# Two decoder layers over a cached attention: one ring of four equal places for the weights, the first MLP in two column halves, and values that are given up by quarters

## The chip, the core and the metric

The kernel runs on one core of a Trainium2 chip. The core has five engines, each with its own queue of instructions: PE (TensorE, matrix products into PSUM), DVE (VectorE), ACT (ScalarE), POOL (GpSimd) and SP (SyncE), which here only issues transfers. Sixteen DMA engines move data between the chip's memory (HBM) and the on-chip memory (SBUF, 128 partitions). Engines wait for each other, and for transfers, on semaphores.

The metric is the device time of one execution in microseconds. Before the change the median of three runs is 2713.64 us (2713.55 to 2716.07).

## The reference

Two sublayers, an attention over a key and value cache and a gated MLP, are run twice with the same weights and caches:

```python
def _A_ref(x, k_cache, v_cache, wq, wo):          # x: (2, 1, 576); caches: (2, 32, 8192, 128)
    q = (x @ wq).reshape(B, Sq, H, Dh).transpose(0, 2, 1, 3)
    scores = jnp.einsum("bhqd,bhkd->bhqk", q, k_cache) * (Dh ** -0.5)
    p = _softmax(scores, axis=-1)
    o = jnp.einsum("bhqk,bhkd->bhqd", p, v_cache)
    return o.transpose(0, 2, 1, 3).reshape(B, Sq, H * Dh) @ wo

def _B_ref(x, w_gate, w_up, w_down):               # 576 -> 4608 -> 576
    return _gelu(x @ w_gate) * (x @ w_up) @ w_down

x = x + _A_ref(_layernorm(x), ...)
x = x + _B_ref(_layernorm(x), ...)
x = x + _A_ref(_layernorm(x), ...)
x = x + _B_ref(_layernorm(x), ...)
```

Everything is 32-bit float. The caches are 2 x 268 MB and are read in both layers; the weights are about 51 MB a layer.

## The kernel before

**Items.** The 2 x 32 pairs of batch and head are 64 items. An item's keys are 8192 x 128, laid out as 128 partitions of 64 rows each, 32 KB a partition, 4 MB in all; its values the same. The first layer takes the items forward, the second backward. The last two items' keys and the last three items' values stay in SBUF between the layers (`keys_held`, `values_held`, five slots) and are not read again.

**Space.** One tile, `space`, holds all that is loaded: six slots of 8192 columns (32 KB a partition each) and 1024 columns more. `Arena` hands it out while the program is written: `slot` for a whole item, `quarter` for a quarter of one, `ring` for pieces of weights, first fit from the end of the last piece. `cache`, `eighths`, `down`, `out_rows` and `products` put loads into one list, `queue`, in the order of use; `pump` issues the head of the list on SP as soon as the planner finds room for it, and stops where it does not. `done` frees a piece and pumps. SP then waits at run time until the old contents have been used, and everything behind it in the list waits too.

**Between the layers.** With five slots held, the first layer's output projection and MLP and the second layer's W_q have only the last slot and the 1024 columns, 9216 columns in all, from `RING` on. Pieces there are 2304 columns (W_o; gate and up, 9216 bytes a partition), 1728 (W_down in thirds, three rows of 576) and 2048 (W_q). So four to five pieces are loaded ahead.

**Attention** (`attention`, line 370). For item n, DVE multiplies a quarter of the keys by the query in place (line 413), POOL folds it in half (417), DVE adds it up (422) and the quarter is given up (`done`, 430). `peak` (436, a transpose on PE), `highest` (442) and `softmax` (448, 451) belong to item n - 1 and are written between the quarters of item n; then `total` (457) and `values` (472, 32 matmul instructions in the profile), after which the four quarters of the value slot are given up together. In the second layer the third item's keys go by quarters into the ring's slot as the W_q pieces there are used up, and the fourth's and fifth's by quarters into the two held key slots; all others are loaded whole.

**MLP** (`mlp`, line 575). All gate pieces, then all up pieces, each of four and a half rows a partition in nine pieces, accumulate into two banks of PSUM (line 584), columns being spread over four groups of partitions and two banks. Then the results are scaled by the norm's factor (591, 592), spread by 18 small matmuls with a selecting matrix so that hidden units lie on partitions (598), activated (605 to 610) and written to `hT` (612). Then W_down goes piece by piece (620) into `xps`, and x is updated (367). `norm` (341 to 364) stands ahead of each sublayer.

In the second layer the weights may use all of `space` (`weights_at[1]` is 0), so they are loaded far ahead.

Of the kernel before, what the change touches and what calls it, by code (L numbers as in the profile page):

```python
# [15 lines left out]
P = 128  # L16
# [15 lines left out]
EG = DF // 8  # L32
HG = EG // 2
# [7 lines left out]
END = NSLOT * SLOT + 1024  # L41
RING = 5 * SLOT
HELD = 5


class Arena:


    def __init__(self):
        self.live = {}  # L50
        self.freed = [0] * (NSLOT + 1)
        self.clock = 0
        self.at = RING

    def clear(self, lo, n):
        return all(hi <= lo or l >= lo + n for l, hi in self.live.values())

    def slot(self, key, allowed):

        for s in sorted(allowed, key=lambda s: self.freed[s]):  # L60
            if self.clear(s * SLOT, SLOT):
                for k in range(4):
                    self.quarter(key, s * SLOT, k)
                return s * SLOT
        return None

    def quarter(self, key, at, k):
        lo = at + k * PART
        if not self.clear(lo, PART):
            return False  # L70
        self.live[key, k] = (lo, lo + PART)
        return True

    def ring(self, key, n, lo, hi=None):

        for at in [self.at, lo] + sorted(end for _, end in self.live.values()):
            if lo <= at and at + n <= (hi or END) and self.clear(at, n):
                self.live[key] = (at, at + n)
# [12 lines left out]
def decode_layers(ctx, tc, x_in, kc, vc, wq, wo, wg, wu, wd, out):  # L91
# [23 lines left out]
    queue, ready, slots = [], {}, {}  # L115

    def pump():
        while queue:
            t = queue[0][1]()
            if t is None:  # L120
                return
            ready[queue.pop(0)[0]] = t
# [5 lines left out]
    def cache(key, src, hb, allowed, pieces=1, where=None):  # L128

        rows = src[hb % B, hb // B].rearrange("(p j) d -> p j d", p=P)  # L130

        def load(at, lo, hi):
            t = space[:, at:at + SLOT].rearrange("p (j d) -> p j d", d=DH)
            nc.sync.dma_start(t[:, lo:hi, :], rows[:, lo:hi, :])
            return t

        def make():
            at = arena.slot(key, allowed)
            if at is None:
                return None  # L140
            slots[key] = at
            for lo in range(0, J, J // pieces):
                t = load(at, lo, lo + J // pieces)
            return t

        def make_quarter(k):
            at = slots[key] = RING if where == "ring" else slots[where]
            return load(at, k * JC, (k + 1) * JC) if arena.quarter(key, at, k) else None

        if where is None:  # L150
            queue.append((key, make))
        else:

            for k in ((NU + i) % 4 if where == "ring" else i for i in range(4)):
                queue.append((key, lambda k=k: make_quarter(k)))

    def eighths(key, w, us, width, lo, hi=None):

        n = 4 * len(us)

        def make():
            at = arena.ring(key, n * width, lo, hi)
            if at is None:
                return None
            t = space[:, at:at + n * width].rearrange("p (c w) -> p c w", c=n)
            src = w.rearrange("r (e w) -> (r e) w", w=width).rearrange("(p j) w -> p j w", p=P)
            nc.sync.dma_start(t, src[:, 4 * us[0]:4 * us[0] + n, :])
            return t

        queue.append((key, make))  # L170


    ONE = [range(u, u + 1) for u in range(NU)]
    THREE = [range(u, u + 3) for u in range(0, NU, 3)]
    PIECES = {
        ("wq", 0): THREE, ("wq", 1): ONE, ("g", 0): ONE, ("u", 0): ONE, ("g", 1): THREE, ("u", 1): THREE[:-1] + ONE[-3:],
    }

    def down(key, t0, lo, hi, first):

        def make():
            at = arena.ring(key, (hi - lo) * D, first)
            if at is None:
                return None
# [478 lines left out]
```

## Time and profile before

| | |
|---|---|
| median of the runs | 2713.64 us |
| the profiled execution, its own time | 2714.15 us |
| its span, first to last instruction | 2712.4 us |
| mean granted TensorE clock | 0.651 |
| busy: PE, DVE, POOL, ACT | 1144.8, 1887.3, 1209.4, 82.6 us |
| read from HBM | 1154.23 MB |

The profile comes from one execution. An engine is busy while it runs an instruction that computes; waiting and issuing are not counted. The page cuts the span into forty slices of 67.8 us and gives for each the busy tenths and the data rate. A table of stretches gives the same for any part of the span. In a timeline, each row has its start and length in us, the engine, the line of the kernel, what was done and how often, and in brackets the idle time of the engine before it and what ended it. "space<-in_B_w_up_dram" reads: into `space`, from the tensor of the up weights.

### The profile page before, as it was taken

The page shows a single profiled execution, that of the slowest core. Times are in us where ns is not written, and L with a number is a line of the kernel's source. Part 1 is how long each engine was busy: PE and PEld are TensorE (multiplying, and loading weights), DVE is VectorE, ACT ScalarE, POOL GpSimd, SP SyncE. Part 2 cuts the span into 40 slices and gives each one's busy share as a digit, 9 for nine tenths or more (in the row PEclk, how much of TensorE's full clock was granted, in tenths as well). Part 3 has the DMA queues.
Part 4 walks back from the last instruction along what each step waited for, and adds up shares of the span by engine and source line. Part 5 has one row for each costly group of instructions (what it writes and reads, how often), then busy time and mean ns, then how long its engine had stood idle before and what let it go on. Part 6 is the DMA issues. An engine that isn't in the chain of part 4 may idle for free.

```text
span 2712.4 us, 19378 instructions
## 1 busy us (share of the span) xinstructions
PE 1144.8 (42%) x7392; PEld 406.0 (15%) x7392; DVE 1887.3 (70%) x1809; ACT 82.6 (3%) x391; POOL 1209.4 (45%) x522
## 2 busy tenths in 40 slices
PE   2344434343434343444555434343434343434356
PEld 0111111111111111111211111111111111111122
DVE  5777777777777777776039877777777777777740
ACT  0000000000000000000000000000000000000000
POOL 3545454444445454443016554444444454445420
PEclk7666666666666666666757766666666666566667
DMA  9999999999999999999999999999999999999998
GB/s 418 432 433 431 431 430 431 432 432 431 430 432 432 431 431 431 431 432 414 404 358 409 430 431 432 432 431 430 431 431 432 431 430 431 432 431 431 432 426 378
DMA packets 49099, 1155.48 MB, mean 426 GB/s; under 512 B 5464, under 2 KB 5488, under 8 KB 7664
## 3 DMA queue, kind: packets, MB, share of 16 engines
q1 hardware_dynamic: 48968, 1154.24, 99.4%
q8 instruction: 58, 0.95, 0.1%
q14 instruction: 33, 0.27, 0.0%
q10 hardware_dynamic: 40, 0.01, 0.0%
HBM read 1154.23 MB, written 0.00 MB: 426 GB/s over the span
## 4 chain that ended last, share of the span: by engine, by line
DMA 80%; DVE 10%; PE 8%; issue 2%; POOL 0%; ACT 0%; DVEq 0%; POOLq 0%; SPq 0%; ACTq 0%
DMA space<-in_A_k_cache_dram 45%; DMA space<-in_A_v_cache_dram 28%; PE acc L472 7%; DVE space L413 5%; DVE S L422 3%; DMA space<-in_B_w_down_dram 2%; DMA space<-in_B_w_gate_dram 2%; DMA space<-in_A_wo_dram 1%; DMA space<-in_B_w_up_dram 1%; DMA space<-in_A_wq_dram 1%; DVE osb L489 1%; PE xps L620 0%; PE acc L584 0%; PE acc L377 0%; POOL space L417 0%
## 5 line engine op out<-in xcount | busy, mean ns | idle before, releaser
L417 POOL TENSOR_TENSOR space<-space 128x1024 f32<-128x1024 f32 x512 | 1206.4, 2356 | 1257.1 <-DVE space L413 1221.7
L413 DVE TENSOR_TENSOR space<-space,qp 128x2048 f32<-128x2048 f32 x512 | 1164.7, 2275 | 483.8 <-DMA space<-in_A_k_cache_dram 460.9
L472 PE MATMUL acc<-space,prz 128*8 128x512 f32 x4096 | 727.4, 874 | 290.1 <-DVE osb L489 170.6
L422 DVE TENSOR_REDUCE S<-space 128x16 f32<-128x1024 f32 x512 | 615.9, 1203 | 3.3 <-POOL space L417 3.3
L438 PE MATMUL mT<-ident,m 128*1 128x128 f32 x128 | 46.7, 365 | 794.2 <-DVE m L436 794.2
L472 PEld LDWEIGHTS acc<-space,prz 128*8 128x8 f32 x4096 | 133.7, 115 | 771.4 <-issue 723.5
L444 PE MATMUL nb<-m,ones 1*128 1x1 f32 x256 | 74.1, 356 | 254.8 <-DVE m L442 254.8
L438 PEld LDWEIGHTS mT<-ident,m 128*1 128x1 f32 x128 | 10.1, 79 | 820.0 <-DVE m L436 814.0
L457 PE MATMUL tot<-rs,ones 128*128 128x1 f32 x256 | 74.7, 361 | 92.7 <-ACT prz L451 92.7
L444 PEld LDWEIGHTS nb<-m,ones 1*128 1x128 f32 x256 | 63.1, 305 | 291.4 <-DVE m L442 291.4
L448 ACT ACTIVATE nbs<-nb 128x1 f32<-128x1 f32 x128 | 21.9, 171 | 2359.9 <-PE nb L444 2359.9
L503 DVE TENSOR_TENSOR oT<-po,rinv 32x16 f32<-32x16 f32 x64 | 10.9, 170 | 110.7 <-PE po L498 110.7
L363 POOL TENSOR_TENSOR rstd<-ve,mhalf 128x1 f32<-128x1 f32 x4 | 2.2, 552 | 174.0 <-DVE ve L361 174.0
L457 PEld LDWEIGHTS tot<-rs,ones 128*128 128x128 f32 x256 | 63.7, 309 | 104.0 <-ACT prz L451 103.5
L396 PE MATMUL qp<-qsb,pick 4*128 4x128 f32 x256 | 62.3, 325 | 27.9 <-DVE space L413 24.8
L584 PE MATMUL acc<-space,xt 128*8 128x288 f32 x576 | 56.3, 545 | 39.9 <-DMA space<-in_B_w_up_dram 19.9
L489 DVE SCALAR_TENSOR_TENSOR osb<-acc,diag,osb 128x128 f32<-128x128 f32 x192 | 67.3, 351 | 6.8
L592 DVE TENSOR_SCALAR o<-acc,rstd 128x288 f32<-128x288 f32 x2 | 1.0, 516 | 94.1 <-ACT o L591 94.1
L396 PEld LDWEIGHTS qp<-qsb,pick 4*128 4x128 f32 x256 | 38.0, 186 | 88.1 <-PE acc L472 48.5
L367 DVE TENSOR_TENSOR x<-xps,x 128x144 f32<-128x144 f32 x4 | 1.2, 308 | 70.8 <-PE xps L620 42.1
L498 PEld LDWEIGHTS po<-of,osb 128*32 128x32 f32 x512 | 40.1, 151 | 49.1 <-issue 39.6
L451 ACT ACTIVATE prz<-S,nbs 128x64 f32<-128x64 f32 x128 | 44.6, 348 | 4.4 <-ACT nbs L448 0.4
(56 smaller groups left out, 332.0 us busy)
## 6 DMA issues: line engine op xcount, KB each, us to landing
space<-in_A_k_cache_dram SPq DMA_DIRECT2D x123, 4096.0 KB
space<-in_A_v_cache_dram SPq DMA_DIRECT2D x123, 4096.0 KB
space<-in_A_wo_dram SPq DMA_DIRECT2D x16, 1152.0 KB
space<-in_B_w_up_dram SPq DMA_DIRECT2D x12, 1152.0 KB
space<-in_A_k_cache_dram SPq DMA_DIRECT2D x12, 1024.0 KB
space<-in_B_w_down_dram SPq DMA_DIRECT2D x13, 864.0 KB
space<-in_B_w_gate_dram SPq DMA_DIRECT2D x9, 1152.0 KB
space<-in_B_w_gate_dram SPq DMA_DIRECT2D x3, 3456.0 KB
```

Source lines behind the costliest of these rows:

```text
L396: nc.tensor.matmul(qb[n], pick[32 * c:32 * c + 4, r:r + 1].to_broadcast([4, P]), qsb[32 * c:32 * c + 4, (h % 4) * DH:(h % 4 + 1) * DH], st ...
L413: nc.vector.tensor_tensor(out=u, in0=t, in1=qb[n].unsqueeze(1).to_broadcast([P, JC, DH]), op=ALU.mult)
L417: nc.gpsimd.tensor_tensor(out=half, in0=half, in1=u[:, :, DH // 2:], op=ALU.add)
L422: nc.vector.tensor_reduce(out=S[n][:, k * JC:(k + 1) * JC], in_=prod.pop((n, k)), axis=AX.X, op=ALU.add)
L438: nc.tensor.transpose(mT[n], m, ident)
L444: nc.tensor.matmul(mT[n], ones[0:1, :], m1, start=True, stop=True)
L451: nc.scalar.activation(pr, S.pop(n).rearrange("p (g r) -> p g r", r=4), AF.Exp, bias=nbs, scale=scale, accum_out=rs[n],)
L457: nc.tensor.matmul(tot, ones, rs.pop(n), start=True, stop=True)
L472: nc.tensor.matmul(acc[32 * c:32 * c + 8, (n // B) % 2, :], prz[:, n % 3, at:at + 8], t[:, 4 * g:4 * g + 4, :].rearrange("p j d -> p (j d) ...
L489: nc.vector.scalar_tensor_tensor(t, q[:, r, :], diag[:, r:r + 1], t, op0=ALU.mult, op1=ALU.add,)
L498: nc.tensor.matmul(po[lo:lo + 32, i, :], t[:, i::GH], of, start=True, stop=True)
L584: nc.tensor.matmul(acc[32 * c:32 * c + 4 * B, s, :HG], xt[:, 32 * u + at:32 * u + at + 4 * B], w[:, 4 * (u - us[0]) + c, s * HG:(s + 1) * HG],
```

## The change

**The ring** is now four places of 2304 columns (`PLACE`, `NPLACE`), taken in turns by whatever comes, W_o, gate and up, W_down, W_q and the third item's key quarters (`Arena.ring`). `fit` keeps the old first fit for the first W_q and for the second layer's later weights. W_down goes in pieces of four rows, and the ninth rows of all four groups go in one last piece.

**The first MLP** is done in two column halves. A half's gate and up rows go in nine places: four of gate, one mixed of gate and up, four of up. Two of the nine rows that belong to a pair of partitions are loaded by one transfer to the even partitions and one to the odd ones (`t[e::2]`), each of 64 rows of 9216 bytes; the mixed place takes four transfers of 64 rows of 4608 bytes. `norm(split=True)` arranges x to match. A half has one bank of `acc`. `activate` replaces the spreading matmuls with a transpose on DVE; it is written once for each half, the first one ahead of the second half's products. In the second layer the products are as before, then both halves are activated, then W_down.

**The second attention.** `values` gives up a quarter after each four groups of matmuls. The keys of item 4 and the values of item 3 (counted from 0, in the order of use) are loaded by quarters in a mixed order, the values into the quarters that item 0's values give up; item 5's keys go by quarters into item 1's value slot. For n = 1, `highest` and `softmax` of item 0 stand ahead of the second `multiply` instead of behind it.

```diff
+PLACE = DF // 2
+NPLACE = 4
 RING = 5 * SLOT
+END = RING + NPLACE * PLACE
...
+    def ring(self, key, n):
+        at = self.take(key, RING + self.turn % NPLACE * PLACE, n)
+        self.turn += at is not None
+        return at
...
+    def split_rows(name, w, h, u):
+        rows = w[:, DF // 2 * h:DF // 2 * (h + 1)].rearrange("(m r) w -> m r w", r=NU)
+        def transfers(t):
+            for e in range(2):
+                nc.sync.dma_start(t[e::2, :], rows[:, 5 * e + u, :])
+        weights((name, 0, h, u), DF // 2, None, transfers)
+
+    def split_middle(h):
+        def transfers(t):
+            for g, w in enumerate((wg, wu)):
+                for e in range(2):
+                    lo, n = DF // 4 * (2 * h + e), DF // 4
+                    nc.sync.dma_start(
+                        t[e::2, n * g:n * (g + 1)], w[:, lo:lo + n].rearrange("(m r) w -> m r w", r=NU)[:, 4, :]
+                    )
+        weights(("gu", 0, h), DF // 2, None, transfers)
...
+    DOWN = [
+        [[(t, i) for i in range(lo, lo + 4)] for t in range(NT) for lo in (0, 4)] + [[(t, NI - 1) for t in range(NT)]],
...
+            if layer and n == 4:
+                for turn, k in (("k", 0), ("v", 0), ("v", 1), ("k", 1), ("v", 2), ("v", 3), ("k", 2), ("k", 3)):
+                    if turn == "k":
+                        cache_quarter(key, kc, hb, k, ("k", 1, seq[1]))
+                    else:
+                        cache_quarter(("v", 1, seq[3]), vc, seq[3], k, ("v", 1, seq[0]))
+            elif layer and n in (2, 3, 5):
+                for k in range(4):
+                    cache_quarter(key, kc, hb, k, {2: "ring", 3: ("k", 1, seq[0]), 5: ("v", 1, seq[1])}[n])
...
-    def norm():
+    def norm(split=False):
...
+        if split:
+            xm = xs[:, :5 * 32].rearrange("p (u m e) -> p u m e", u=5, e=2)
+            parts = [(xm[:, 0:4, :, e], xr[:, 5 * e:5 * e + 4, :], 0) for e in range(2)]
+            parts += [(xm[:, 4, :, e], xr[:, 4, :], e) for e in range(2)]
+            xs = xs[:, :5 * 32].rearrange("p (u q) -> p u q", u=5)
...
             for g in range(J // 4):
...
+                if left and g % 4 == 3:
+                    done((key, g // 4))
...
+            soon = layer == 1 and n == 1
+            if soon:
+                highest(n - 1)
+                softmax(n - 1)
             multiply(n, 1)
-            if before:
+            if before and not soon:
                 highest(n - 1)
                 softmax(n - 1)
...
+        def split_products(h):
+            steps = [(("g", layer, h, u), u, 2, (0,)) for u in range(4)] + [(("gu", layer, h), 4, 1, (0, 1))]
+            steps += [(("u", layer, h, u), u, 2, (1,)) for u in range(4)]
+            for key, u, sides, gs in steps:
+                w = ready.pop(key).rearrange("p (k c w) -> p k c w", c=4, w=HG)
+                for k in range(2):
+                    g, e = (k, 0) if u == 4 else (gs[0], k)
+                    for c in range(4):
+                        nc.tensor.matmul(
+                            acc[32 * c:32 * c + 4 * B, h, :HG], window(u, 4 * g + 2 * e), w[:, k, c, :],
...
+        def activate(v):
+            o = once.tile([P, 2, HG], F32, name="o", tag="row")
+            nc.scalar.activation(o[:, 0, :], acc[:, v, :HG], AF.Copy, scale=rstd)
+            gu = o[:, 1, :].rearrange("p (i r) -> p i r", i=NI)
+            nc.vector.transpose(gu, o[:, 0, :].rearrange("p (m i) -> p i m", i=NI))
+            g = gu[:, :, 0:4]
+            a = once.tile([P, NI, 4], F32, name="ga", tag="part")
+            nc.vector.tensor_mul(a, g, g)
+            nc.vector.tensor_scalar(a, a, 0.044715, 1.0, op0=ALU.mult, op1=ALU.add)
+            nc.vector.tensor_mul(a, a, g)
+            nc.scalar.activation(a, a, AF.Tanh, scale=math.sqrt(2.0 / math.pi))
+            nc.vector.scalar_tensor_tensor(a, a, 1.0, g, op0=ALU.add, op1=ALU.mult)
+            nc.vector.tensor_mul(a, a, gu[:, :, 4:8])
+            a, to = a.rearrange("p i (e b) -> p (i e) b", b=B), hT[:, v].rearrange("p i e s b -> p (i e) s b")
+            nc.vector.tensor_scalar_mul(to[:, :, 0, :], a, 0.5)
+            nc.scalar.mul(to[:, :, 1, :], a, 0.5)
+
+        if not split:
+            all_products()
+        for v in range(2):
+            if split:
+                split_products(v)
+            activate(v)
```

321 lines of the change are left out of this document (147 added, 174 removed).

## The prediction

> **What bounds the kernel now.** I read the page first: the span, the row of forty slices, the bytes and the shares of the chain that ended last.
>
> ```profile
> span 2712.4 us, 19378 instructions
> DMA  9999999999999999999999999999999999999998
> GB/s 418 432 433 431 431 430 431 432 432 431 430 432 432 431 431 431 431 432 414 404 358 409 430 431 432 432 431 430 431 431 432 431 430 431 432 431 431 432 426 378
> HBM read 1154.23 MB, written 0.00 MB: 426 GB/s over the span
> DMA 80%; DVE 10%; PE 8%; issue 2%; POOL 0%; ACT 0%; DVEq 0%; POOLq 0%; SPq 0%; ACTq 0%
> ```
>
> The transfers are the bound. In the two attentions they run at 431 to 432 GB/s, slice after slice, and no engine's time shows. The change reads the same bytes, so it can win only where the transfers stand still or run thin. Apart from the two ends, that is slices 19 to 22, the weights between the attentions and the second attention's start. The next view is the table of stretches there (time, then PE, PEld, DVE, ACT and POOL busy, the granted clock, the share of the DMA engines in use, GB/s).
>
> ```profile
> 1285.00:1290.00 5.00, 4.43 (x72) 2.66 (x72) 0.66 (x3) 0.00 (x0) 0.00 (x0) 0.51 0.67 230
> 1320.00:1340.00 20.00, 12.62 (x116) 2.82 (x112) 0.00 (x0) 0.00 (x0) 0.00 (x0) 0.67 1.01 425
> 1350.00:1365.00 15.00, 9.56 (x164) 6.12 (x156) 2.01 (x8) 0.77 (x2) 0.00 (x0) 0.61 0.76 276
> 1365.00:1380.00 15.00, 10.61 (x168) 4.67 (x168) 0.00 (x0) 0.00 (x0) 0.00 (x0) 0.54 1.01 419
> 1385.00:1395.00 10.00, 6.63 (x40) 0.44 (x32) 0.00 (x0) 0.00 (x0) 0.00 (x0) 0.67 0.98 381
> 1410.00:1425.00 15.00, 1.69 (x5) 1.07 (x5) 14.70 (x12) 0.00 (x0) 10.62 (x6) 0.50 0.75 270
> 1425.00:1426.00 1.00, 0.27 (x3) 0.24 (x2) 1.00 (x2) 0.61 (x3) 1.00 (x1) 0.50 0.68 287
> 1426.00:1427.00 1.00, 1.00 (x6) 0.38 (x10) 1.00 (x1) 0.00 (x0) 0.63 (x1) 0.50 0.67 139
> 1425.00:1435.00 10.00, 6.34 (x37) 1.74 (x36) 10.00 (x8) 0.61 (x3) 6.80 (x4) 0.76 0.82 292
> 1436.00:1446.00 10.00, 6.96 (x39) 2.24 (x38) 10.00 (x9) 0.61 (x3) 6.59 (x4) 0.66 1.02 423
> ```
>
> With a full queue, the ring stage streams 425 GB/s (1320 to 1340). Against that, the loss of a stretch is its length times the missing share:
> - 1285 to 1290: 5 x 195/425 = 2.3 us;
> - 1350 to 1365: 15 x 149/425 = 5.26 us;
> - 1385 to 1395: 10 x 44/425 = 1.0 us;
> - 1410 to 1425: 15 x 155/425 = 5.5 us;
> - 1425 to 1435: 10 x 133/425 = 3.1 us.
>
> Together that is 17 us, 0.6% of the run, and the most that the whole change can regain. From 1436 on the queue is full again.
>
> **The first MLP in two halves (1350 to 1365).** The timeline of this place:
>
> ```profile
> 1332.07 1.16 PE L584 MATMUL acc<-space,xt 128*8 128x288 f32 x16 [1.62 <-DMA space<-in_B_w_up_dram]
> 1334.85 2.11 PE L584 MATMUL acc<-space,xt 128*8 128x288 f32 x16 [1.63 <-DMA space<-in_B_w_up_dram]
> 1350.93 0.33 SPq L187 DMA_DIRECT2D space<-in_B_w_down_dram  x1
> 1351.06 0.50 ACT L591 ACTIVATE o<-acc,rstd 128x288 f32<-128x288 f32 x1 [79.40 <-PE acc L584]
> 1356.16 0.37 DVE L612 SCALAR_TENSOR_TENSOR hT<-ga,gu 128x72 f32<-128x72 f32 x2
> 1356.59 6.30 PE L620 MATMUL xps<-space,hT 128*4 128x144 f32 x120 [2.07 <-DVE hT L612]
> 1357.31 0.33 SPq L187 DMA_DIRECT2D space<-in_B_w_down_dram  x1
> ```
>
> Each piece of 1152 KB lands 2.78 us after the one before (1332.07 to 1334.85), and PE uses it in 1.16 to 2.11 us, so PE always waits for the transfer. After the last piece the order turns round. Activating takes from 1351.06 to 1356.59, 5.5 us. In that time PE frees no place, and SP, which issued at 1350.93, issues next at 1357.31: 6.4 us without an issue into a ring that holds about 11 us. The queue runs dry.
>
> After the change, half 0 is activated under the nine places of half 1 (9 x 2.78 = 25 us of transfers). PE goes straight from the last product of half 1 to the W_down rows of half 0, which are four places (t = 0 and 1), 11.1 us of transfers. Half 1's activation lies under those. Its length comes from these groups:
>
> ```profile
> L357 DVE STREAM_TRANSPOSE xt<-xc 128x288 f32<-128x288 f32 x1 | 0.7, 690 | 0.0
> L591 ACT ACTIVATE o<-acc,rstd 128x288 f32<-128x288 f32 x1 | 0.5, 502 | 79.4 <-PE acc L584 79.4
> L598 PE MATMUL gu<-spread,o 128*64 128x16 f32 x36 | 2.4, 282 | 1.3 <-DVE o L592 1.3
> L606 DVE TENSOR_TENSOR ga<-ga 128x72 f32<-128x72 f32 x1 | 0.2, 232 | 0.0
> L609 ACT ACTIVATE ga<-ga 128x72 f32<-128x72 f32 x1 | 0.3, 263 | 4.0 <-DVE ga L608 4.0
> ```
>
> The new chain is one copy (0.50), one transpose of 288 columns (0.69), six small DVE steps on half the elements (at most 0.23 each, 1.4) and a tanh (0.26): 2.9 us, 3.1 with the gaps; the 2.4 us of spreading matmuls are gone. Eleven microseconds cover three, so I take the whole **-5.26 us**. Without the cover (below), about half of it stays.
>
> The second MLP also activates in two halves, one after the other, 6.2 us in place of 5.5. That lies under W_down pieces already free to stream: in the second MLP, PE waits for its last large piece anyway.
>
> ```profile
> 2702.79 6.68 PE L620 MATMUL xps<-space,hT 128*4 128x144 f32 x144 [3.78 <-DMA space<-in_B_w_down_dram]
> ```
>
> Cost nothing; with that 3.78 us gone it would be 0.7. The split norm swaps two subtractions for four shorter ones and transposes 160 columns for 288: nothing, under the four first gate places in flight.
>
> **What this half costs.** Each gate or up place now takes two transfers of 64 rows, and the mixed place four. SP needs 0.33 us for an issue (rows above), 1.3 us for the worst place against 2.78 us: hidden. For a row's fixed cost I compare rates. At 432 GB/s a row of 32 KB takes an engine 1.214 us (32768 x 16/432), at 425 a row of 9 KB 0.347; a line through both leaves 8 ns per row. The two mixed places add 256 rows. K and V in quarters in place of two whole loads add 768, and W_down in rows of 9216 bytes in place of 6912 saves 128. That is 896/16 x 8 ns = **+0.45 us**. There are 24 more transfers (22 from the two halves, 6 from the quarters, less 4 of W_down). Taking one more small write per engine at that same price, **+0.2 us** (bounds 0 and 0.4).
>
> That price assumes that transfers of 64 rows, at every second partition, stream like those of 128. No row of this trace shows one. From below, nothing beats 432 GB/s: 18 places x 0.05 = 0.9 us gained. From above, the nearest row is 1410 to 1425, where 0.75 of the engines moved 270 GB/s, so half of them would move 180 to 215 and a place would take 5.6 us or more: 18 x 2.78 = 50 us lost. I take the 425 row, since 64 rows still divide by 16 engines and up to four places queue.
>
> The Trainium skill speaks against this edit: "SBUF — State Buffer", section "Summary: rules for kernel authors", says that a DMA-bound transfer should be one DMA over 128 partitions and not several, and "DMA: Bandwidth & Descriptors", section "Bandwidth", has 1 MB transfers at 341 GB/s. By that last figure alone a 1152 KB piece would take 3.5 us, 18 of them 12 us more, and the sum would come to 2720. The trace has 2.78, since the next ones are already queued, so I do not use the figure.
>
> **The ring.** Places are 2304 columns; the old gate and up pieces had the same size, so depth does not change. W_down goes from three rows a piece to four, and its last piece grows.
>
> ```profile
> 1375.33 1.62 PE L620 MATMUL xps<-space,hT 128*4 128x144 f32 x24 [0.40 <-DMA space<-in_B_w_down_dram]
> 1380.09 0.31 DVE L367 TENSOR_TENSOR x<-xps,x 128x144 f32<-128x144 f32 x1 [23.56 <-PE xps L620]
> 1385.11 0.33 SPq L167 DMA_DIRECT2D space<-in_A_wq_dram  x1
> ```
>
> Three rows cost PE 1.62 us, so four rows 2.16 in place of about 0.54 for the last single row: x, the norm and the first W_q matmuls come 1.6 us later. Late next is the fifth W_q transfer, 1385.11 here, 5 us behind the addition. Ahead of it stand four W_q pieces, 1 MB each at 425, 2.5 us, 10 us in all; so most of the 1.6 us is covered. The stretch 1385 to 1395 already loses 1.0 us, though, and some engines run dry there. I take half of that again, **+0.5 us** (bounds -1.0, all regained, and +1.6).
>
> **The second attention's start.** The rows, DVE first:
>
> ```profile
> 1421.79 0.22 DVE L436 TENSOR_REDUCE m<-S 128x1 f32<-128x64 f32 x1
> 1422.06 0.37 PE L438 MATMUL mT<-ident,m 128*1 128x128 f32 x1 [3.86 <-DVE m L436]
> 1424.12 0.27 DVE L442 TENSOR_REDUCE m<-mT 1x1 f32<-1x128 f32 x1
> 1425.54 0.33 SPq L134 DMA_DIRECT2D space<-in_A_k_cache_dram  x1
> 1426.28 5.39 PE L472 MATMUL acc<-space,prz 128*8 128x512 f32 x32
> 1428.93 0.33 SPq L134 DMA_DIRECT2D space<-in_A_k_cache_dram  x1
> 1436.00 0.38 SPq L134 DMA_DIRECT2D space<-in_A_v_cache_dram  x1
> ```
>
> Keys come a quarter at a time, 3.4 us apart (1425.54, 1428.93), at DVE's pace, and carry 2.5 us of transfer each. The value load stands behind four of them on SP and goes out at 1436.00, though the values it replaces were used up at 1426.28 + 5.39 = 1431.7. The change lets value quarters go out between the key quarters, as each four groups of PE free one (5.39/4 = 1.35 us).
>
> Up to 1425.5 nothing changes: the four K quarters before are paced by DVE, and the 5.5 us of 1410 to 1425 stay. The next K quarter still opens the flow, so the thin 1425 to 1427 (138/425 + 286/425 = 1.0 us) stays as well. It grows, because the early maximum and softmax of item 0 make DVE wait: the matrix mT is there at 1422.06 + 0.37 = 1422.43, the maximum takes 0.27, so the second multiply starts at 1422.7 in place of 1421.9 or so, and the K quarter behind it is 0.7 us late. From there two value quarters follow at once and the queue stays full. So 3.1 - 1.0 - 0.7 = 1.4 us come back: **-1.4 us** (bounds -3.1, and +0.7 if the values come too late to fill a gap).
>
> **Sum.** -5.26 + 0.45 + 0.2 + 0.5 - 1.4 = -5.5 us. The profiled execution took 2714.15 us, 1.75 outside its span and 0.5 above the median of the three runs, 2713.64. It becomes 2708.6, and by the median **2708.1 us**. With all terms at their good ends (-5.26 - 3.1 - 1.0 + 0.45 = -8.9) it is 2704.7; at their bad ones (-5.26 + 0.7 + 0.45 + 0.4 + 1.6 = -2.1), 2711.5.
>
> **Rivals.**
>
> (a) *Half transfers run slower*, and the kernel ends slower than before. Place: the 18 gate and up places, 1300 to 1350. Engines that must share a way into the 64 partitions they write at that moment would hold each other up. Against it: each place reaches over all 128 partitions and four are queued; for it: no row shows such a transfer, and 0.75 of the engines gave only 270. It decides from 5.5/18 = 0.31 us a place, 2.78 to 3.1. At twice the time for a place it costs 50 us, 2758; at one and a half, 25 us, 2733. The Trainium skill's "SBUF — State Buffer", section "Door 1: The DMA port swizzle", states that partitions share sixteen ports and that a transfer over the first 64 reaches only eight of them; by its formula, every second partition reaches all sixteen. It does not say how 64 rows are dealt to the engines.
>
> (b) *The hole only gets shorter*: W_down's first rows wait for half 1 after all, because both halves are in one tile. Then a chain of 3.1 us stands where 5.5 stood. The hole's cost falls by 2.4 us at most, the other terms sum to -0.25: 2711.0. For it: PE waited for that tile in the row of 1356.59. Against it: the one tile that holds all keys, values and weights is waited for piece by piece, as the rows of 1332.07 and 1334.85 show.
>
> (c) *The quarters do not fill*: key quarters still set the pace, the early softmax costs its 0.7 us and W_q loses 1.6. Then -5.26 + 0.7 + 0.45 + 0.2 + 1.6 = -2.3: 2711.3.
>
> (d) *More comes back*: turns in equal places also smooth the 2.3 us at 1285 and the 1.0 us at 1385: 2708.1 - 3.3 - 0.5 = 2704.3. Against it: the output rows there wait for the last head, whatever place they take.
>
> **Chances.** Forecast 0.54, (a) 0.29, (b) 0.05, (c) 0.03, (d) 0.09. A measurement of this kernel tells about 0.2% from no change, 5.4 us, so the line is at 2708.2, and the forecast lies on it. I give 0.30 of it to faster and 0.24 to within; with (d), faster 0.39. Within: 0.24 + 0.05 + 0.03 = 0.32. Slower: 0.29. The forecast's own range is 2704.7 to 2711.5. The range for eight in ten goes down to 2703 and up to 2734, past the half-size case of (a); the full-size one is left out.
>
> **What would show it.** Right: the stretch around the first activation at 420 GB/s or more, with no issue gap of 6 us on SP, and W_down's first matmuls directly behind the last up product; each half transfer place landing within 2.8 us of the last; value issues between the key issues of the second attention's fourth step, and 420 GB/s from two microseconds after its first quarter. Wrong: PE waits of over 2 us for the gate and up weights at an even spacing of 3.1 us or more (rival a); PE waiting for hT after the last up product (b); gaps left between those key quarters, or a dry queue at W_q (c).

## The result and the profile after

| | before | after |
|---|---|---|
| median of 16 runs each | 2714.50 us (2711.72 to 2716.07) | 2709.44 us (2707.76 to 2711.35) |
| the profiled execution, its own time | 2714.15 us | 2710.29 us |
| its span | 2712.4 us | 2708.4 us |
| mean granted TensorE clock | 0.651 | 0.648 |
| read from HBM | 1154.23 MB | 1154.23 MB |

The ratio is 0.9981, with a 95% interval of 0.9974 to 0.9988. That is 5.1 us faster, 3.3 to 7.1 by the interval. The gain is clear of zero, but at 0.19% it is about as small as the line of 0.2% on which the forecast of 2708.1 lay. One execution of the changed kernel among the runs below, of 3071.47 us at another granted clock (1.0), is left out of all figures.

The page of the changed kernel, the rows that were shown of the page before:

```profile
span 2708.4 us, 19293 instructions
...
DMA  9999999999999999999999999999999999999998
GB/s 418 433 432 430 431 433 432 430 431 432 431 431 431 432 430 432 431 431 421 397 374 419 431 431 431 432 431 430 431 431 432 432 430 430 432 430 432 430 428 378
...
HBM read 1154.23 MB, written 0.00 MB: 426 GB/s over the span
...
DMA 78%; DVE 11%; PE 8%; issue 2%; POOL 0%; another core or an unknown queue 0%; SPq 0%; ACT 0%; DVEq 0%; POOLq 0%; ACTq 0%
```

Only slices 19 to 22 moved by more than 3 GB/s: 414, 404, 358, 409 became 421, 397, 374, 419. Three are better and one, the 20th, is worse. The table of stretches says where. First some rows of the kernel before that the prediction did not need (time, then PE, PEld, DVE, ACT and POOL busy, the granted clock, the share of the DMA engines in use, GB/s):

```profile
1300.00:1320.00 20.00, 10.90 (x114) 3.37 (x114) 2.33 (x8) 0.00 (x0) 0.56 (x1) 0.76 1.01 416
...
1345.00:1365.00 20.00, 11.92 (x188) 6.89 (x188) 2.01 (x8) 0.77 (x2) 0.00 (x0) 0.66 0.83 313
...
1380.00:1390.00 10.00, 6.38 (x34) 0.88 (x34) 2.41 (x8) 0.00 (x0) 0.55 (x1) 0.66 1.01 402
```

And the same stretches of the changed kernel:

```profile
1300.00:1320.00 20.00, 12.46 (x130) 3.94 (x122) 2.43 (x10) 0.00 (x0) 0.55 (x1) 0.67 0.95 370
1320.00:1340.00 20.00, 12.12 (x120) 3.07 (x112) 1.84 (x7) 0.97 (x3) 0.00 (x0) 0.71 1.01 423
1345.00:1365.00 20.00, 12.39 (x196) 5.45 (x200) 1.84 (x7) 0.97 (x3) 0.00 (x0) 0.73 1.01 421
...
1380.00:1390.00 10.00, 7.03 (x40) 1.06 (x40) 1.07 (x4) 0.00 (x0) 0.55 (x1) 0.68 0.93 347
1405.00:1425.00 20.00, 5.03 (x23) 2.16 (x27) 19.23 (x14) 0.61 (x3) 14.07 (x6) 0.50 0.76 274
1425.00:1435.00 10.00, 4.18 (x23) 0.82 (x15) 9.96 (x9) 0.00 (x0) 7.04 (x3) 0.67 0.97 406
```

The hole at the first activation is gone (313 became 421), transfers of 64 rows stream at 423 where those of 128 had 425, and the second attention's start rose from 292 to 406. Lower than before are the first gate pieces (416, now 370) and the W_q pieces (402, now 347).

To price the places I added up the landed bytes in the transfer records of each trace and took the time at which a given amount was in. All amounts are the same in both kernels, so the differences between the columns are gains and losses. "Before, again" and "after, again" are second executions of the two kernels, of the runs below. In us against the first trace of before:

| landed, MB | place | before, again | after | after, again |
|---|---|---|---|---|
| 551 | before the last W_o pieces | 0.0 | 0.0 | +0.2 |
| 557 | W_o in | -0.45 | -0.7 | +0.2 |
| 578 | up pieces of the first MLP | +0.7 | +1.8 | +2.2 |
| 584 | W_down begun | -0.3 | -3.4 | -2.9 |
| 605 | W_q in | -0.95 | -2.3 | -2.1 |
| 632 | second attention's first items | -0.9 | -3.8 | -3.6 |
| 1150 | the end | -0.9 | -3.9 | -3.6 |

From the first trace of before to that of after: +1.8 from the last W_o pieces to the end of the halves, -5.2 at the activation, +1.1 at W_q, -1.5 in the second attention, together -3.8. Behind 632 MB nothing changes any more. The second column is a warning: two executions of one kernel differ by 0.9 us here, and by up to 1.2 from one row to the next.

### The profile page after: what moved, and what is told of

It reads as the page before. It is cut to its first block, busy times and chain, and to the rows that moved or that the text cites. A ratio compares the mean times of both kernels' runs of the same rounds, so it can differ in the third digit from the quotient of the medians.

```text
span 2708.4 us, 19293 instructions
## 1 busy us (share of the span) xinstructions
PE 1136.5 (42%) x7320; PEld 401.7 (15%) x7320; DVE 1889.6 (70%) x1807; ACT 84.7 (3%) x399; POOL 1208.8 (45%) x522
## 3 DMA queue, kind: packets, MB, share of 16 engines
HBM read 1154.23 MB, written 0.00 MB: 426 GB/s over the span
## 4 chain that ended last, share of the span: by engine, by line
DMA 78%; DVE 11%; PE 8%; issue 2%; POOL 0%; another core or an unknown queue 0%; SPq 0%; ACT 0%; DVEq 0%; POOLq 0%; ACTq 0%
DMA space<-in_A_k_cache_dram 45%; DMA space<-in_A_v_cache_dram 23%; PE acc L521 7%; DVE space L461 6%; DVE S L470 3%; DMA space<-in_A_wo_dram 3%; DMA space<-in_B_w_up_dram 3%; DMA space<-in_B_w_down_dram 2%; DMA space<-in_A_wq_dram 1%; DVE osb L537 1%; PE acc L426 0%; DMA space<-in_B_w_gate_dram 0%; POOL space L465 0%; PE acc L646 0%; DVE m L490 0%
## 5 line engine op out<-in xcount | busy, mean ns | idle before, releaser
L546 PE MATMUL po<-of,osb 128*32 128x2 f32 x512 | 37.6, 195 | 6.6 <-DVE osb L537 6.6
```

The costliest lines, as they stand in the source:

```text
L546: nc.tensor.matmul(po[lo:lo + 32, i, :], t[:, i::GH], of, start=True, stop=True)
```

## The experiments

Each is compared with runs of the kernel before on the same chip, and the ratio is to these. Where a version stands on the changed kernel, a ratio of 0.998 means that nothing was lost. The intervals are about 2.4 us wide to either side, so that most verdicts below rest on the stretches of the traces and on the landed bytes.

**The changed kernel again**, unchanged.

> The changed kernel once more, to see which of the differences between the two traces come back. Theory: against the kernel before, the hole at the first activation (5.3 us) is gone, about 1.4 us come back at the second attention's start, and 1.5 to 2.5 us are lost where the first mixed gate-and-up place is loaded (1305 to 1315), in all 4 to 5 us faster, 0.9981 to 0.9985. Rival: the loss at 1305 to 1315 belongs to that one execution; then the stretch runs at 410 GB/s or more here.

Measured: 2709.28 us, 0.9983 [0.9974, 0.9992]; its column stands in the table above. The gain comes back, and so do the losses at the halves (377 GB/s from 1300 to 1320) and at W_q.

**The kernel before again**, unchanged.

> The kernel before once more, for a second trace. Theory: the first one had a full clock for the last W_o group (1.16 us where all later runs have 2.10), so its norm came 1 us early by chance; here x is updated near 1301 and 1300 to 1320 carries 385 to 400 GB/s in place of 416, and the execution is about 1 us longer. Rival: the changed kernel's own order slows that group; then 1299.9 and 416 come back.

Measured: 2713.17 us in one execution. The last W_o group in the timelines of the first trace of before, of the changed kernel and of this second trace of before, and then the stretch that follows in the last one (in a timeline: start, length, engine and line; in brackets the wait before it):

```profile
1298.68 1.16 PE L515 MATMUL xps<-space,oT 128*4 128x144 f32 x32 [1.72 <-DMA space<-in_A_wo_dram]
```

```profile
1298.81 2.10 PE L563 MATMUL xps<-space,oT 128*4 128x144 f32 x32 [0.74 <-DMA space<-in_A_wo_dram]
```

```profile
1298.85 2.10 PE L515 MATMUL xps<-space,oT 128*4 128x144 f32 x32 [0.76 <-DMA space<-in_A_wo_dram]
```

```profile
1300.00:1320.00 20.00, 12.88 (x130) 3.95 (x122) 2.42 (x8) 0.00 (x0) 0.55 (x1) 0.67 0.96 392
```

The same 32 matmuls took 1.16 us in the first trace of before and 2.10 in the second, and the stretch behind them has 392 in place of 416. So a good part of the loss at the first gate pieces, 24 of the 46 GB/s, is not the change's.

**The activation of both halves after all products.** If the overlap with half 1 is what closes the hole, about half of it should come back by the prediction.

```diff
         for v in range(2):
             if split:
                 split_products(v)
+        for v in range(2):
             activate(v)
```

> Both halves are activated after both halves' products, so nothing lies under the first half's activation any more. Theory: two chains of 3.1 us, 5.5 to 6.2 us, stand between the last up product and W_down again, SP stops issuing for about 6 us, and the 5.3 us of the hole come back: 2714 to 2715.5, slower than the changed kernel by 4.5 to 6. Rival: the gain came from the ring's even places; then the time stays within 1.5 us of 2709.4.

Measured: 2710.21 us, 0.9986 [0.9977, 0.9994]; 410 GB/s from 1345 to 1365, where the changed kernel has 421. That is 20 x 11/421 = 0.5 us. SP paused for 5.2 us between two issues, from 1352.00 to 1357.18, and yet the queue did not run empty. With W_down pieces of four rows the overlap is hardly needed.

**No halves**: the changed ring and pieces, and the second attention, but gate and up in the old order, both halves activated afterwards.

```diff
-            for h in range(2):
-                for u in range(4):
-                    split_rows("g", wg, h, u)
-                split_middle(h)
-                ...
+            for name, w in (("g", wg), ("u", wu)):
+                for us in single:
+                    half_rows((name, 0, us[0]), w, us, None)
...
-        split = layer == 0
+        split = False
...
-                for us in GU[g]:
+                for us in GU[g] if layer else single:
```

> The changed kernel without its column halves: gate and up of the first MLP go as in the second one, all products and then both activations, but in the ring's equal places, one transfer of 128 rows a place. Theory after the late activation: the larger, even places of W_down alone carry the queue over the activation, and the transfers of 64 rows only cost; so 1345 to 1365 stays at 410 GB/s or more, 1300 to 1320 returns to 405 or more, and the time is 1 to 2 us below the changed kernel, 2707.5 to 2708.5. Rival (the prediction's): without the halves the hole of 5.3 us comes back, 2714 to 2715.

**W_down in fours alone**: the kernel before, and only the pieces of its first W_down changed from three rows to four.

```diff
+    DOWN[0] = [(t, lo, lo + 4) for t in range(NT) for lo in (0, 4)] + [(t, NI - 1, NI) for t in range(NT)]
```

> The kernel before with one edit: the first layer's W_down in pieces of four rows (2304 columns) instead of three (1728), the ninth rows one by one. Theory: the hole came from four pieces of three rows lying in the ring, 8.3 us of transfers, where four of four rows are 11.1; then 1350 to 1365 rises from 276 to 370 GB/s or more and the time falls by 3 to 4.5 us, to 2709.5 to 2711. Rival: the 5.5 us of activation empty either; then the stretch stays below 320 and the time at 2713 to 2714.

Measured: without halves 2709.43 us, 0.9984 [0.9975, 0.9992]; with fours alone 2713.07 us, 0.9995 [0.9986, 1.0004]. Without halves 1345 to 1365 kept its 411 GB/s, so the prediction's hole did not come back; 1300 to 1320 rose only to 386, not to 405, and the time stayed where it was. With fours alone 1350 to 1365 rose from 276 to 360 GB/s, a little short of the 370 expected and well above the rival's 320, but only 1.0 us was gained in place of 3 to 4.5. The next two turn it round.

**Halves with W_down in thirds**, and **no halves with thirds**:

```diff
-        [[(t, i) for i in range(lo, lo + 4)] for t in range(NT) for lo in (0, 4)] + [[(t, NI - 1) for t in range(NT)]],
+        [[(t, i) for i in range(lo, lo + 3)] for t in range(NT) for lo in (0, 3, 6)],
```

> The changed kernel with its column halves, but the first layer's W_down in pieces of three rows as before, each in a place of its own (8.3 us of transfers in four places). Theory: the halves alone close the hole too, since PE goes on from the last up product to W_down without a stop; 1345 to 1365 at 410 GB/s or more, the time within 1 us of the changed kernel. Rival: the closing needs the pieces of four rows; then the stretch falls below 390 and 2 us or more are lost.

> The kernel without halves (all products, then both activations), with W_down in pieces of three rows. Theory: with 8.3 us in the ring and a gap of about 5 us on SP, part of the hole comes back, as far as the shorter chain (3.1 us to the first W_down in place of 5.5) does not cover it: 345 to 395 GB/s in 1345 to 1365, 1.5 to 3 us slower than with four rows. Rival: the shorter chain alone closes it; then the stretch stays at 405 or more.

Measured: with halves 2709.93 us, 0.9985 [0.9976, 0.9995]; without 2711.14 us, 0.9991 [0.9982, 1.0], 1.7 us above no halves with fours.

The transfers' view of the stretch 1345 to 1366 shows the hole in each, in forty slices of 0.525 us. The kernel before:

```profile
GB/s 474 360 426 417 434 413 421 421 421 426 395 408 408 408 356 382 395 408 316 145 53 26 0 0 0 224 145 355 408 421 237 184 197 303 387 329 342 421 408 435
```

Fours alone:

```profile
GB/s 456 421 421 439 404 439 404 439 404 456 382 456 369 456 404 474 369 474 386 456 386 456 386 456 369 228 176 70 263 123 246 456 386 456 386 330 263 386 404 369
```

No halves, thirds (the shorter chain alone):

```profile
GB/s 369 492 351 492 338 448 404 421 404 421 421 439 395 408 408 421 408 356 355 421 421 303 145 118 53 158 171 290 421 421 356 145 237 342 382 329 408 408 434 426
```

No halves, fours (both):

```profile
GB/s 404 439 404 439 404 439 404 456 386 474 382 439 369 474 351 492 351 492 351 492 351 527 334 509 334 439 298 439 351 456 404 316 369 369 439 421 351 456 400 404
```

The changed kernel:

```profile
GB/s 421 439 404 439 404 439 404 439 421 439 421 421 421 439 404 439 417 421 386 421 386 456 386 456 386 456 404 439 404 439 404 439 404 453 386 421 386 456 386 456
```

Before, the flow stops for some 3 us from the 20th slice on, and thins again in the 31st to 33rd. Fours push the gap back by six slices, since four of them last longer, and a shorter chain narrows it; with both, no slice falls below 298. As a loss over the 20 us from 1345 to 1365 (20 x missing share of 425), one trace to a figure; the second one for no halves with fours is that of the early output projection below:

| W_down's rows may be used | thirds | fours |
|---|---|---|
| 5.5 us after the products (old chain) | 313 and 333 GB/s: 5.3, 4.3 us | 377: 2.3 us |
| 3.1 us after (new chain, no halves) | 350: 3.5 us | 411 and 399: 0.7, 1.2 us |
| at once (halves) | 404: 1.0 us | 421: 0.2 us |

So fours alone lacks two things of the change: the hole keeps 2.3 us, and the second attention its 1.5. That does not explain all of its time: its hole gained 2.0 to 3.0 us on the two traces of before, its landed bytes are 2.4 us ahead at 605 MB and 1.6 at 632, and its median is 1.0 ahead, within the interval.

**The mixed places last**, so that no transfer of 4608-byte rows stands in the middle. `split_middle(h)` moves behind the up rows, in the plan and in the products.

```diff
                 for u in range(4):
                     split_rows("g", wg, h, u)
-                split_middle(h)
                 for u in range(4):
                     split_rows("u", wu, h, u)
+                split_middle(h)
```

> The mixed place, four transfers of 288 KB, goes last in each half instead of fifth. Theory: it cost about 2 us because its four issues of half a microsecond each came when the queue was just dry after the norm; moved to where the queue is full it costs nothing, and 1300 to 1320 returns to 405 GB/s or more, 1.5 to 2 us faster than the changed kernel (about 2707.6). Rival: all transfers of 64 rows refill a dry queue slowly, mixed or not; then the stretch stays at 370 to 385 and the time at 2709.4.

Measured: 2709.10 us, 0.9982 [0.9973, 0.9991]; 375 GB/s from 1300 to 1320, against 370. The mixed places are not what thins that stretch. The rival's condition fits: all six traces with halves on SP's queue and a last W_o group of 2.10 us have 370 to 377 GB/s there, and the five without halves and with the same 2.10 us have 379 to 392.

**Half of the issues on ACT's queue**, since SP needs longer for a transfer of 64 rows, as the row below has it for the changed kernel, than the 0.33 us of a whole one:

```profile
1320.69 0.47 SPq L198 DMA_DIRECT2D space<-in_B_w_gate_dram  x1
```

```diff
             for e in range(2):
-                nc.sync.dma_start(t[e::2, :], rows[:, 5 * e + u, :])
+                (nc.sync, nc.scalar)[e].dma_start(t[e::2, :], rows[:, 5 * e + u, :])
```

(and the same in `split_middle`)

> The transfers to the odd partitions are issued on the ACT queue, so that a place's two transfers are issued side by side and SP's half microsecond for each no longer adds up. Theory: the slow refill after the first norm is the issue, 1300 to 1320 rises to 395 GB/s or more and 1 to 1.5 us are gained, about 2708.3. Rival: the refill is late because the first place is given up late; then the stretch stays at 370 to 380 and the time within 1 us of 2709.4.

Measured: 2712.90 us, 0.9997 [0.9988, 1.0006], 3.5 us above the version without halves, measured beside it; neither the theory nor the rival had that. The row of its last W_o group, and then the stretch behind it:

```profile
1300.82 2.10 PE L563 MATMUL xps<-space,oT 128*4 128x144 f32 x32 [2.90 <-DMA space<-in_A_wo_dram]
```

```profile
1300.00:1320.00 20.00, 12.19 (x130) 4.25 (x130) 2.44 (x10) 0.00 (x0) 0.55 (x1) 0.67 0.89 321
```

PE waited 2.90 us for W_o in place of 0.74. Gate transfers issued by ACT no longer stand behind the W_o pieces on SP's queue; they share the engines with them, and W_o, needed first, comes 2 us later. The Trainium skill's "DMA: Bandwidth & Descriptors", section "Issuing engines are not separate DMA queues", says that transfers of any issuer run on the same sixteen engines and interleave; these rows agree.

**The last W_down piece in two**, so that the last group's matmuls wait for one row only.

```diff
-        ... + [[(t, NI - 1) for t in range(NT)]],
+        ... + [[(t, NI - 1) for t in range(NT - 1)], [(NT - 1, NI - 1)]],
```

> The first layer's last W_down piece, the four ninth rows, becomes two places of three rows and one. Theory: x and the norm come 1.1 to 1.6 us earlier after the last landing, and 1380 to 1390 rises from 347 to 385 GB/s or more, 0.5 to 1 us gained (2708.4 to 2708.9). Rival: the next place being only a quarter full makes the ring thinner by as much; then the time stays within 0.4 us of 2709.4.

Measured: 2709.31 us, 0.9982 [0.9973, 0.9991]. The stretches around W_q:

```profile
1365.00:1380.00 15.00, 9.81 (x162) 4.97 (x154) 1.92 (x7) 0.00 (x0) 0.00 (x0) 0.66 1.00 387
1380.00:1390.00 10.00, 5.68 (x36) 0.93 (x40) 0.49 (x2) 0.00 (x0) 0.55 (x1) 0.83 0.97 374
```

The first has 387 where the changed kernel has 415, the second 374 where it has 347: the loss only moves. That the place with a single row is the reason, as the rival has it, fits this and was not tested apart.

**The second attention as before**, with the rest of the change.

```diff
-            elif layer and n in (2, 3, 5):
+            if layer and n in (2, 3, 4):
...
-            if not (layer == 1 and (held or n == 3)):
+            if not (layer == 1 and held):
...
-            soon = layer == 1 and n == 1
+            soon = False
```

> The second attention loads and orders as before: item 3's values and item 5's keys whole, the early maximum and softmax taken out. Theory: the quarters are worth 1 to 1.5 us, so 2710.4 to 2711, with 280 to 310 GB/s in the ten microseconds after the first quarter of item 4's keys. Rival: the quarters fill nothing that is not lost again to the shorter rows; then it stays at 2709.4 or falls below.

Measured: 2710.72 us, 0.9988 [0.9979, 0.9997]; 1425 to 1435 is back at 311:

```profile
1425.00:1435.00 10.00, 5.37 (x35) 1.14 (x27) 9.97 (x9) 0.00 (x0) 6.89 (x3) 0.84 0.87 311
```

From 605 to 632 MB this trace gains 0.05 us on the first trace of before, and the changed kernel gains 1.5.

**An earlier output projection**, a try at the 2.3 us of 1285 to 1290, on the version without halves: the middle groups of W_o are multiplied ahead of the last head's outputs.

```diff
         gather(H - 1)
+        for g in others[:-1]:
+            project(g)
         context(H - 1)
         divide(H - 1)
-        for g in others:
-            project(g)
+        project(others[-1])
```

> The kernel without halves, and in both layers the output projection's groups 2 to 6 go ahead of the last head's gathering matmuls instead of behind them; they do not need the last head. Theory: the loss of 2.3 us at 1285 to 1290 comes from PE waiting for the last head's gather before it gives up W_o places; projecting first lets SP issue about 2 us earlier, 1285 to 1300 rises from 355 to 385 GB/s or more and 1.5 to 2 us are gained, about 2707.5. Rival: the first norm then waits for the same last landing and the ring is as dry a few microseconds later; then the time stays within 0.7 us of 2709.4.

Measured: 2708.71 us, 0.9981 [0.9973, 0.999], the lowest median of all, but not to be told from 2709.4; 1285 to 1300 has 369 GB/s, not 385. PE was ready earlier and then waited for the transfer:

```profile
1284.78 2.10 PE L560 MATMUL xps<-space,oT 128*4 128x144 f32 x32 [1.78 <-DMA space<-in_A_wo_dram]
```

## Why the prediction was right, point by point

**The hole** (-5.26): measured -5.2 against the first trace of before and -4.2 against the second, whose own hole was smaller. The size held. PE went on almost as described; the rows of the changed kernel:

```profile
1351.81 0.50 ACT L669 ACTIVATE o<-acc,rstd 128x288 f32<-128x288 f32 x1 [23.14 <-PE acc L646]
...
1353.33 1.16 PE L695 MATMUL xps<-space,hT 128*4 128x144 f32 x32 [1.64 <-DVE ga L674]
...
1354.54 0.23 ACT L682 ACTIVATE hT<-ga 128x36 f32<-128x36 f32 x1 [0.49 <-DVE ga L679]
...
1356.15 2.10 PE L695 MATMUL xps<-space,hT 128*4 128x144 f32 x32 [1.66 <-DMA space<-in_B_w_down_dram]
```

Half 1's chain lasts from 1351.81 to 1354.77, 3.0 us (3.1 predicted), and PE began with W_down at 1353.33, before the last row of that chain had run. The profile puts the 1.64 us before it down to DVE, but the first W_down piece was all in only at 1353.20. In the second trace it was in at 1353.33, and PE began at 1353.46, when half 1's transpose had run for 0.02 us. So W_down's first rows wait for their transfer and not for half 1. Rival (b) is out.

But the reason was only half right, and "without the cover, about half of it stays" was wrong: 0.5 us stays of 5. The step that failed is "a ring that holds about 11 us", which was meant of the kernel before. Its W_down pieces were thirds of 864 KB; by its own row of 425 GB/s one takes 2.08 us, and the four behind the last up piece 8.3. Four pieces of 1152 KB hold 11.1 us. And not even that much lies there when SP stops. By the transfer records, this is what was still to land at SP's last issue, at 425 GB/s, and the time until the next issue:

| | still to land | until the next issue | loss in the hole |
|---|---|---|---|
| before, its two traces | 4.2, 5.2 us | 6.4, 6.4 us | 5.3, 4.3 us |
| no halves, thirds | 4.3 us | 4.75 us | 3.5 us |
| fours alone | 7.9 us | 7.75 us | 2.3 us |
| halves, thirds | 5.9 us | 3.7 us | 1.0 us |
| no halves, fours | 7.3 us | 5.2 us | 0.7 us |
| the changed kernel | 7.9 us | 3.8 us | 0.2 us |

The loss goes with the difference of the two. So the hole had three cures in the change, each enough by itself for a part: larger pieces (from 4.8, the mean of two, to 2.3), a shorter chain (4.8 to 3.5), the overlap (with thirds, 3.5 to 1.0). Two of them leave little for the third. I had named the overlap alone.

**The cost of the halves** (+0.2 and 256 of the 896 rows, 256/16 x 8 ns = 0.13, in all 0.33): over six traces with halves and a 2.10 us last W_o group, 551 to 578 MB costs 1.5 to 2.0 us against the first before, 1.7 in the mean; over five without halves and with the same 2.10 us, the kernel before again among them, 0.7 to 1.6, in the mean 1.1. So the halves cost some 0.6 us, somewhat above the forecast and far from rival (a). It is not spread over the 18 places: from 1320 to 1340 the stream has 423 or 424 GB/s with halves and 423 to 425 without. It falls in 1300 to 1320, where the queue fills again behind the norm (370 to 377 against 379 to 392, which is 20 x 12/425 = 0.6 us at the means). Why two transfers fill it more slowly than one is not shown. The prediction quoted the Trainium skill against this edit, "SBUF — State Buffer", section "Summary: rules for kernel authors": one transfer over 128 partitions and not several. In the full queue of 1320 to 1340 two in place of one lose nothing that these traces can show. The Trainium skill's "DMA: Bandwidth & Descriptors", section "Why a DMA increments its semaphore by 16 and not by 1", speaks against rival (a): a transfer is dealt to the largest number of engines up to sixteen that divides its rows, so 64 rows use all of them, as 128 do. The 423 GB/s agree. The prediction had the division by 16 and gave that rival 0.29 all the same.

**W_q** (+0.5, bounds -1.0 to +1.6): x came later than its data, as described; how much of that is lost is less clear. The chain that starts the second attention, in the timeline of the kernel before:

```profile
1402.20 1.89 PE L377 MATMUL acc<-space,xt 128*4 128x512 f32 x8 [0.60 <-DMA space<-in_A_wq_dram]
...
1405.81 4.48 DVE L413 TENSOR_TENSOR space<-space,qp 128x2048 f32<-128x2048 f32 x2 [22.67 <-PE qp L396]
```

In the changed kernel, with the last W_down piece and the addition to x ahead of it:

```profile
1375.64 2.10 PE L695 MATMUL xps<-space,hT 128*4 128x144 f32 x32 [0.81 <-DMA space<-in_B_w_down_dram]
1377.84 0.31 DVE L416 TENSOR_TENSOR x<-xps,x 128x144 f32<-128x144 f32 x1 [23.11 <-PE xps L695]
...
1399.77 1.89 PE L426 MATMUL acc<-space,xt 128*4 128x512 f32 x8 [0.59 <-DMA space<-in_A_wq_dram]
...
1403.38 4.49 DVE L461 TENSOR_TENSOR space<-space,qp 128x2048 f32<-128x2048 f32 x2 [22.27 <-PE qp L445]
```

The data were 3.4 us early when the last W_down piece was in (587 MB), x only 2.25 (1380.09 to 1377.84), since that piece now takes PE 2.10 us (2.16 predicted). The last W_q matmuls start 2.43 us early, and so does DVE's first product, which sets the pace of the keys: in all the twelve other traces of which I added up the bytes, the gain at 605 MB is that of this first product within 0.25 us. So 3.4 - 2.43 = 1.0 us is lost here, in the second trace of the changed kernel 0.8. The term was 0.5: in these two traces less of the late x is covered by the four pieces ahead than I took, for the first product comes 25.54 us behind the update of x in the changed kernel and 25.72 before. Over all fourteen traces that distance goes from 24.0 to 26.1 us, though, and that is more than the term. In the version without halves it turned into a gain:

```profile
1375.79 1.16 PE L692 MATMUL xps<-space,hT 128*4 128x144 f32 x32 [1.41 <-DMA space<-in_B_w_down_dram]
1377.04 0.31 DVE L413 TENSOR_TENSOR x<-xps,x 128x144 f32<-128x144 f32 x1 [19.51 <-PE xps L692]
...
1398.61 1.04 PE L423 MATMUL acc<-space,xt 128*4 128x512 f32 x8 [0.75 <-DMA space<-in_A_wq_dram]
...
1401.06 4.49 DVE L458 TENSOR_TENSOR space<-space,qp 128x2048 f32<-128x2048 f32 x2 [20.97 <-PE qp L442]
```

Both the W_down piece and the last W_q piece are 0.9 us shorter there, at the same work. Late activation, with a W_down piece of 1.16 us too, gains 0.8 between 587 and 605 MB. Mixed places last gains 0.3 with a piece of 2.10 us, so that piece is not all that decides. Halves with thirds lost 0.6 although x, at 1376.90, was nearly as early as its data (3.2 and 3.3 us). So the runs do not show the term as this edit's own; it stays open.

**The second attention** (-1.4, less the fixed cost of its 768 rows, 768/16 x 8 ns = 0.38, so -1.0): measured -1.5 in both traces. The timeline of SP shows the value quarters between the key quarters:

```profile
1424.16 2.03 SPq L136 DMA_DIRECT2D space<-in_A_v_cache_dram  x2
1427.06 0.33 SPq L136 DMA_DIRECT2D space<-in_A_k_cache_dram  x1
1427.56 1.19 SPq L136 DMA_DIRECT2D space<-in_A_v_cache_dram  x2
1430.38 3.65 SPq L136 DMA_DIRECT2D space<-in_A_k_cache_dram  x2
```

The key quarter ahead of them went out at 1423.67, 4.32 us behind the last one at 1419.35; before, it was 3.76 (1421.78 to 1425.54), and with the old second attention 3.77. So the early softmax cost 0.56 us, predicted 0.7. Two microseconds behind that quarter the queue is full, 423 GB/s from 1425.7 to 1435.7. The thin stretch ahead of it stayed, as said: 274 GB/s from 1405 to 1425 (306 before, where it begins 2.4 us later). Rival (c) is out, and the version with the old second attention shows the 1.5 us as this part's own.

**Rival (d)** was not seen: 1285 to 1300 has 366 and 344 GB/s in the two traces of the changed kernel and 347 and 361 in those of before, the landed bytes behind W_o (557 MB) differ as much between executions of one kernel as between the kernels, 1380 to 1390 got worse, and the early projection met the transfer.

**The sum.** The forecast was -5.5, and the runs gave -5.1. That it came so close is in part luck: the interval is 3.8 us wide, the first pair of traces has +1.8 where 0.3 was forecast, and the hole closed for more reasons than the one that I had given. The traces gave -3.9 and, second against second, -2.7, which lies outside the interval of the runs. Late activation and no halves, whose medians are those of the changed kernel, end 5.5 and 6.3 us ahead of the first before in their traces, largely by the W_q chain. So a pair of traces can be some 2 us off the medians; that this is the whole difference was not shown.

## What to carry to other kernels

When a queue of loads runs dry at a serial stage, write down first what the queue will still hold, in us, at its last issue before that stage, with the sizes of the very pieces that lie in it, and set it against the time until the next issue: here 4.2 or 5.2 us against 6.4, where I had taken 11. A one-line change of the piece took half of the hole away, without restructuring the products. Then look for the cheapest cure; the column halves, for which the products were rearranged, cost 0.6 us and closed 0.5 to 1.0 us beyond what larger pieces and a shorter chain bring. And before a difference of 1 us between two traces is put down to an edit, profile the unchanged kernel a second time.

## What the hardware showed that was not expected

**The clock inside a chain.** The same 32 matmuls took 2.10 us where the granted clock was 0.50 and 1.16 where it was 1.00. Here the changed kernel and then the version without halves, in the stretch of the last W_down piece:

```profile
1375.60:1377.70 2.10, 2.06 (x32) 1.02 (x32) 0.00 (x0) 0.00 (x0) 0.00 (x0) 0.50 0.99 414
```

```profile
1375.70:1377.00 1.30, 1.16 (x32) 0.75 (x32) 0.00 (x0) 0.00 (x0) 0.00 (x0) 1.00 1.01 410
```

The means over the whole executions are 0.648 and 0.652, so the mean hides it. Which of the two a short piece gets changes from one execution to the next, and moves what hangs on it by 0.9 us.

**The issue of a transfer of 64 rows** takes SP 0.47 to 0.60 us in 36 of the 40 cases of the changed kernel, up to 1.32 in the others; that of a place of 128 rows takes 0.33, which the prediction had used for both. In the full stream it was hidden, as two issues, four for a mixed place, stand against 2.78 us. A second queue to relieve SP cost 3.5 us, and the late W_o shows why: the order between the transfers was given up.
